# Gated mix of softmax attention and a linear-attention branch: the fraction step of VectorE's score batches on GpSimd, apart from two-port VectorE operations, and a new order

## The chip, the cores and the metric

The kernel runs on one core of one Trainium2 chip. The metric is the device time of one execution in microseconds (us). Before the change the median of three runs is 838.36 us (837.57 to 838.61). Stretches of the program are read from one profiled execution.

## The reference, cut to what matters

Sequence S = 2048, width 512, 32 heads of 16 numbers, bf16 inputs.

```python
qkv = x @ wqkv                                  # branch A, per head q, k, v
p = softmax(einsum("bhqd,bhkd->bhqk", q, k) * Dh ** -0.5)
a = einsum("bhqk,bhkd->bhqd", p, v) @ wo

phi = lambda u: concat([softmax(u @ w_phi), softmax(-(u @ w_phi))])   # branch B
kv, z = einsum("bhsf,bhsd->bhfd", phi(k), v), sum_s(phi(k))
b = (einsum("bhqf,bhfd->bhqd", phi(q), kv) / (phi(q) . z + 1e-6)) @ wo_B

g = sigmoid((x * gate_w).sum(-1))
out = g * a + (1 - g) * b
```

Nearly all of the work is branch A: 32 heads of 2048 x 2048 scores, an exponential of each, and the product with v.

## The kernel before, in words

**Tiles and packs.** The scores are cut into 2048 units: a unit is one head, 128 keys by 512 queries. Four units (four heads, on four row groups of TensorE) are a pack; 512 packs run in order, in 32 groups of 16 packs (the 16 key blocks of four heads and one query chunk). One pack lasts about 1.6 us.

**Two ways for the exponential.** Most units go the ScalarE way: `_qk` (L1001) writes their scores into a ring of five PSUM banks, `_exp` (L1027, the activation at L1035) takes 3 and 2 units by turns and writes ET, and `_pv` (L1042, L1104) multiplies ET with V. The units in `self.away` go the VectorE way. `_plan_vector` (L831) chooses them: SHARES[g] of them in group g, spread over the 14 packs behind the group's first (in the last group over ENDS places), always the fourth head of a pack; four more (SOON) are fixed by hand. They are gathered in batches of NB = 5 (the first two have 2, the last ones fewer).

**A batch on VectorE** (`_vector_batch`, L862): per unit a score matmul (`vqk`) into one of three PSUM banks outside the ring, and an evacuation `v_bits` (L883) that scales the scores into uint32 in the tile vt, which has two buffers. Then, for all units of the batch at once, `_cubic` (L902): `v_frac` (L907) takes one byte of each number, a fraction, into vf as fp16; `v_line` (L909), `v_sq` (L910) and `v_cube` (L911) make a cubic polynomial of it; and `v_out` (L893) adds the exponent and writes bf16 bits into vu. TensorE multiplies vu with V in a step of its own (`pvx`, L1104, vu).

**Other work of VectorE.** Evacuations of projections (L703, L759, L783, L1252, L1268), the norm of each pair of groups (L1157 to L1169), all of branch B's feature map (`_b_part`, L1255, names b_...), and the output (L1489, L1541). GpSimd (the engine POOL) does nothing but a few fills and small steps in the first 24 us.

**What sets the order.** All operations are listed with an engine, a planned cost, dependencies, a due time in packs (`prio`) and an earliest time (`rel`). `Plan.order` (L153) plays them through in Python ahead of time with its planned costs and latencies, and picks for the engine that is ready first the operation that is due first. The result is one fixed instruction queue for each engine; `emit` (L286) puts semaphore waits where a dependency crosses engines. At run time each engine works through its queue in order, so an instruction that waits holds all that stand behind it. TensorE's queue also holds padding matmuls (`_fill`, L1109, recorded at L1113) where it would have little to do.

`self.n_bits % 2` chooses the vt buffer. LEAD is by how many packs a batch is due ahead of its first use, QDUE the same for the query projections (`_proj_q`, L751: a projection, an evacuation at L759 and eight small DMAs on SP's queue into qT), K0 and Q0 the start of branch B's key and query steps, KEEP the pack of a group from which a bank is held back for the next group's accumulator.

## Time and profile before

| | us |
|---|---|
| median of three runs | 838.36 |
| span of the profiled execution | 836.5 |
| TensorE busy | 792.9 |
| VectorE busy | 806.8 |
| ScalarE busy | 825.4 |
| GpSimd busy | 8.0 |
| first score activation starts, last one ends | 7.35, 831.64 |
| granted TensorE clock, mean | 1.000 |

The span runs from the first to the last instruction of the profiled execution; it is 1.86 us under the median of the runs. In the lines below, PE is TensorE, PEld its weight loads, DVE is VectorE, ACT is ScalarE, POOL is GpSimd, SP the engine that issues most DMAs. A group line gives the line of the code, engine, operation, output <- input, shapes and count, then the busy time and the mean time of one in ns, then how long the engine sat idle just before these instructions and what ended that. A line of a stretch gives its bounds, its length and then for PE, PEld, DVE, ACT and POOL the busy time and the number of instructions. A timeline line gives start and length in us. Instructions that follow each other on an engine overlap a little in these records: one that reads PSUM on VectorE is listed with 0.68 us while the next starts 0.60 us later.

### The profile page before, as it was taken

Reading aid. Unit: us, or ns where it says so; the run is one execution under the profiler, and the core shown is the slowest. Engines: PE = TensorE matmul, PEld = TensorE weight load, DVE = VectorE, ACT = ScalarE, POOL = GpSimd, SP = SyncE. Lnnn points to the kernel's source line nnn. Section 1 sums busy time; section 2 is a strip of 40 time slices with the busy share of each in tenths; the row PEclk is TensorE's granted clock in tenths of the full one; section 3 lists DMA queues with packets and bytes.
Section 4 is the critical chain, followed back from the end, with each engine's and each line's share of the span. In section 5 each row is a group of like instructions: output and inputs, shape, how many; then the busy total and the mean of one; then the engine's idle time right before and its main releaser. Section 6 shows DMA issues by size and latency. Waiting matters only on the chain.

```text
span 836.5 us, 19540 instructions
## 1 busy us (share of the span) xinstructions
PE 792.9 (95%) x8711; PEld 263.0 (31%) x8753; DVE 806.8 (96%) x1050; ACT 825.4 (99%) x733; POOL 8.0 (1%) x15
## 2 busy tenths in 40 slices
PE   9999999999999999999999999999999999999998
PEld 4323333333232222232223322222322223222234
DVE  6999999999999999999999999999998999999994
ACT  7999999999999999999999999999999999999997
POOL 3000000000000000000000000000000000000000
PEclk9999999999999999999999999999999999999999
DMA  9500000000000000210003010003100003000000
GB/s 250 157 6 8 1 7 1 2 1 8 2 7 2 7 1 8 52 22 13 1 7 59 20 33 2 4 5 70 27 15 8 1 11 79 21 8 2 2 2 27
DMA packets 49027, 20.01 MB, mean 24 GB/s; under 512 B 38704, under 2 KB 48944, under 8 KB 48944
## 3 DMA queue, kind: packets, MB, share of 16 engines
q1 hardware_dynamic: 48272, 18.58, 9.4%
q8 instruction: 68, 1.11, 0.6%
q10 hardware_dynamic: 672, 0.20, 0.1%
q14 instruction: 15, 0.12, 0.0%
HBM read 6.31 MB, written 2.10 MB: 10 GB/s over the span
## 4 chain that ended last, share of the span: by engine, by line
ACT 92%; DVE 5%; PE 2%; DMA 0%; SPq 0%; issue 0%
ACT ET L1035 92%; DVE vt L883 1%; PE ps L984 0%; DMA qT<-qraw 0%; SPq L761 0%; PE ps L633 0%; DVE vu L893 0%; PE ps L1113 0%; DVE bq L1268 0%; DVE vt L1321 0%; DVE VB L1252 0%; DVE T L1157 0%; DVE vf L907 0%; DVE vu L911 0%; DVE vf L910 0%; DVE bq L1315 0%
## 5 line engine op out<-in xcount | busy, mean ns | idle before, releaser
L1035 ACT ACTIVATE ET<-ps 128x1536 bf16<-128x1536 f32 x728 | 823.1, 1397 | 1.7 <-PE ps L984 1.5
L984 PE MATMUL ps<-qT,kT 32*128 32x512 bf16 (+2 forms) x2249 | 318.4, 364 | 31.4 <-ACT ET L1035 22.2
L1113 PE MATMUL ps<-kT,zero 128*32 128x512 bf16 (+1 forms) x3052 | 255.3, 383 | 0.0
L1104 PE MATMUL ps<-ET,V 128*32 128x512 bf16 (+2 forms) x1998 | 195.8, 364 | 1.3 <-ACT ET L1035 0.6
L984 PEld LDWEIGHTS ps<-qT,kT 32*128 32x128 bf16 x2249 | 83.5, 91 | 305.5 <-ACT ET L1035 227.1
L883 DVE TENSOR_SCALAR vt<-ps 128x512 uint32<-128x512 f32 x226 | 148.3, 681 | 3.8 <-PE ps L984 3.1
L893 DVE SCALAR_TENSOR_TENSOR vu<-vt,vu 128x2560 int16<-128x2560 uint32 (+3 forms) x47 | 127.6, 2716 | 0.7
L1113 PEld LDWEIGHTS ps<-kT,zero 128*32 128x32 bf16 x3052 | 67.9, 94 | 103.2 <-issue 78.5
L1104 PE MATMUL ps<-vu,V 128*32 128x512 bf16 (+1 forms) x250 | 85.3, 364 | 0.3 <-DVE vu L893 0.3
L1104 PEld LDWEIGHTS ps<-ET,V 128*32 128x32 bf16 x1998 | 55.0, 95 | 67.0 <-issue 36.9
L910 DVE TENSOR_TENSOR vf<-vf 128x2560 f16<-128x2560 f16 (+3 forms) x49 | 68.6, 1400 | 0.6
L911 DVE TENSOR_TENSOR vu<-vu,vf 128x2560 f16<-128x2560 f16 (+3 forms) x49 | 68.5, 1398 | 0.5
L907 DVE TENSOR_SCALAR vf<-vt 128x2560 f16<-128x2560 uint8 (+3 forms) x47 | 67.1, 1427 | 0.2
L681 PE MATMUL ps<-WB,xT 128*128 128x512 bf16 x165 | 48.8, 383 | 4.0 <-issue 1.6
L909 DVE TENSOR_SCALAR vu<-vf 128x2560 f16<-128x2560 f16 (+3 forms) x49 | 37.9, 774 | 2.0 <-PE ps L1104 1.8
L681 PE MATMUL ps<-xT,WA 128*128 128x512 bf16 (+1 forms) x124 | 35.8, 380 | 0.0
L1157 DVE STREAM_TRANSPOSE T<-ps 128x512 f32<-128x512 f32 (+1 forms) x35 | 23.2, 664 | 5.0 <-PE ps L1104 4.6
L1104 PEld LDWEIGHTS ps<-vu,V 128*32 128x32 bf16 x250 | 22.9, 96 | 11.5 <-issue 8.5
L681 PEld LDWEIGHTS ps<-WB,xT 128*128 128x128 bf16 x192 | 14.4, 97 | 27.0 <-issue 14.3
L1268 DVE TENSOR_SCALAR bq<-ps 128x512 bf16<-128x512 f32 x32 | 21.5, 679 | 0.5 <-PE ps L681 0.4
L777 PE MATMUL ps<-WA,xT 128*128 128x128 bf16 x256 | 18.9, 220 | 0.4 <-DVE vt L883 0.2
L1321 DVE TENSOR_TENSOR vt<-vt,brec 128x4096 bf16<-128x4096 bf16 (+1 forms) x10 | 18.6, 1857 | 0.0
(105 smaller groups left out, 421.8 us busy)
## 6 DMA issues: line engine op xcount, KB each, us to landing
qT<-qraw SPq DMA_DIRECT2D x120, 16.0 KB, 1.8
xn<-in_A_x_dram SPq DMA_DIRECT2D x3, 512.0 KB, 6.1
WB<-in_B_wqkv_dram SPq DMA_DIRECT2D x3, 512.0 KB, 5.0
out_dram<-WB SPq DMA_DIRECT2D x12, 128.0 KB, 1.9
WA<-in_A_wqkv_dram SPq DMA_DIRECT2D x3, 384.0 KB, 5.2
xn<-in_A_x_dram SPq DMA_DIRECT2D x2, 256.0 KB, 3.6
WoA<-in_A_wo_dram SPq DMA_DIRECT2D x1, 512.0 KB, 5.7
WoB<-in_B_wo_dram SPq DMA_DIRECT2D x1, 512.0 KB, 6.6
```

Of the source, the lines that this page charges most:

```text
L681: mm = op("PE", lambda e, c=c: e.matmul(self._bank(job)[:, 0:n], lhs(c), rhs(c), start=(c == 0), stop=(c == 3)), self.c_pe(n), reads=reads ...
L883: parts.append(op("DVE", lambda e, j=j, job=job: e.tensor_scalar(vt[:, j, :], self._bank(job), SCALE * LOG2E * 2.0 ** 24, 2.0 ** 31, op0=A ...
L893: o = op("DVE", lambda e: e.scalar_tensor_tensor(out=flat(vu).bitcast(I16), in0=flat(vt), scalar=2.0 ** -17, in1=flat(vu), op0=ALU.mult, o ...
L907: ("_frac", two, lambda e: e.tensor_scalar(vf, frac, 1 / 256, ROOT, op0=ALU.mult, op1=ALU.add), [b_vt], [b_vf]),
L909: lambda e: e.tensor_scalar(vu, vf, CUBE, SQUARE, op0=ALU.mult, op1=ALU.add), [b_vf], [b_vu]),
L910: ("_sq", two, lambda e: e.tensor_tensor(vf, vf, vf, ALU.mult), [b_vf], [b_vf]),
L911: ("_cube", two, lambda e: e.tensor_tensor(vu, vu, vf, ALU.mult), [b_vf, b_vu], [b_vu]),
L984: ins = e.matmul(out[u][:, cols], self.kT[32 * i:32 * i + 32, cp, kt * TOK:(kt + 1) * TOK], self.qT[32 * i:32 * i + 32, s, q], start=True, ...
L1035: o = plan.op("ACT", lambda e: e.activation(self.ET[:, a % NS:a % NS + n, :], self.ps[:, a % NR:a % NR + n, :], ACT.Exp, scale=SCALE), sel ...
L1104: ins = e.matmul(self._bank(ot)[32 * i:32 * i + 32, to], self.V[:, kt, g8 // 2, v0:v0 + 32], tile[:, cols], start=first and j == 0, stop=o ...
L1113: ins = e.matmul(self._bank(ot)[32 * i:32 * i + 32, lo:QCH], self.zero[:], self.kT[:, 0, lo:QCH], start=False, stop=False, tile_position=( ...
L1157: return e.transpose(to, acc if alone else acc.rearrange("p (e b d) -> p e b d", e=2, b=8))
```

## The change

Four things change.

1. `v_frac` goes from VectorE to GpSimd in all batches but the two SOON ones and the last two (TAIL). It is the same operation (one byte of each uint32 in, fp16 out), with a planned cost of 0.2 + 0.00138 n us for n numbers. It depends on the `v_out` of the batch before (`last_out`).
2. The planner keeps a set PORT of operation names: those of VectorE that read two tensors from SBUF or copy within SBUF in a fast mode. `order` places no such VectorE operation beside a GpSimd `v_frac`: each gets a dependency, and so a semaphore wait, on the last one of the other engine (GIVE 0.15 and TAKE 0.12 are the planned gaps), and a VectorE operation of the set that would start less than GUARD ahead of a booked `v_frac` is planned behind it. `v_bits`, all other evacuations from PSUM, the 32x32 transposes and the reciprocals are not in the set; `b_octave` (L1321), which reads two SBUF tensors, is not either.
3. The score matmuls of a batch wait for `v_cube` (SOONER) of the batch that last used their vt buffer and no longer for its `v_out`; the evacuation into vt still waits for `v_out`.
4. SHARES sums to 231 instead of 226 and is spread anew; LEAD, QDUE, VPRIO, TPRIO, KEEP, ENDS, K0 and Q0 get new values. With these, and with the new costs, the whole order of all queues is computed anew.

```diff
+    PORT = {"v_frac", "v_line", "v_sq", "v_cube", "v_out", "gate_z", "gate_h", "gate_b", "n_den", "n_mul", "kvbd", "b_grid", "b_rest",
+            "b_max", "b_top", "b_down", "b_square", "b_slope", "b_even", "b_odd", "b_part", "b_out", "b_sum", "b_ratio", "b_mul"}
+    GUARD, GIVE, TAKE = 0.25, 0.15, 0.12
...
+            pool = [(max(free["POOL"], o.dep_t, port["DVE"].end + self.GIVE if port["DVE"] else 0.0), o) for o in avail["POOL"]
+                    if o.port and o.rel <= self.now]
+            booked = min(pool, key=lambda x: x[0]) if pool else None
...
+                    if o.port and e == "POOL" and port["DVE"]:
+                        t = max(t, port["DVE"].end + self.GIVE)
+                    elif o.port and e == "DVE":
+                        if port["POOL"]:
+                            t = max(t, port["POOL"].end + self.TAKE)
+                        if booked and t > booked[0] - self.GUARD:
+                            t = max(t, booked[0] + booked[1].cost + self.TAKE)
...
+            if o.port and e in port:
+                other = port["DVE" if e == "POOL" else "POOL"]
+                if other is not None:
+                    o.deps.append(other)
+                port[e] = o
...
-    NB, NVU, LEAD = 5, 3, 13
-    QDUE, VPRIO, VREL, TPRIO = 28.0, -16.0, 161.0, 5
-    KEEP = 14
+    NB, NVU, LEAD = 5, 3, 14
+    QDUE, VPRIO, VREL, TPRIO = 32.9152, -18.5545, 161.0, 3
+    KEEP = 15
...
-    ENDS = 9
+    ENDS = 11
+    POOL = 0.00138
+    SOONER = "_cube"
+    TAIL = 2
...
-    SHARES = (0, 2, 2, 6, 0, 5, 4, 5, 8, 4, 9, 9, 10, 4, 15, 4,
-              2, 14, 8, 8, 12, 3, 6, 7, 14, 8, 7, 12, 6, 11, 14, 7)
+    SHARES = (0, 2, 2, 8, 0, 5, 5, 2, 9, 4, 11, 8, 12, 3, 13, 4, 4, 11, 7, 11, 8, 6, 8, 10, 14, 6, 4, 14, 6, 10, 14, 10)
...
-                   reads=self._score_bufs([u]), deps=b_vt.readers, name="vqk", prio=due + step * j, rel=due + step * j - self.VREL, kind="row",
+                   reads=self._score_bufs([u]), deps=b_vt.soon or b_vt.readers, name="vqk", prio=due + step * j, rel=due + step * j - self.VREL, kind="row",
...
-                op0=ALU.mult, op1=ALU.add), self.c_dve(512), deps=[m], name="v_bits",
+                op0=ALU.mult, op1=ALU.add), self.c_dve(512), deps=[m, *b_vt.readers], name="v_bits",
...
-            op("DVE", fn, cost, reads=reads, writes=writes, name="v" + name, prio=prio)
-        o = op("DVE", lambda e: e.scalar_tensor_tensor(
+            pool = name == "_frac" and not soon and number < len(self.batches) - self.TAIL
+            o = op("POOL" if pool else "DVE", fn, 0.2 + n * self.POOL if pool else cost, reads=reads, writes=writes, name="v" + name,
+                   prio=prio, deps=[self.last_out] if pool else ())
+            if name == self.SOONER:
+                b_vt.soon = [o]
+        self.last_out = o = op("DVE", lambda e: e.scalar_tensor_tensor(
...
-    K0, SK, Q0, SQ = 17.0, 8.5, 178.25, 18.0
+    K0, SK, Q0, SQ = 16.878, 8.5, 178.0371, 18.0
```

More of the change, by code (lines that the diff above doesn't have):

```diff
@@ L32, in __init__ @@
         self.readers = []
+        self.soon = []
 class Job:
@@ L66, in __init__ @@
         self.strips = (None, ())
+        self.port = name in Plan.PORT
 class Plan:
@@ L165, in order @@
         queues = {e: [] for e in self.ENGS}
+        port = {"DVE": None, "POOL": None}
         left = len(self.ops)
@@ L884, in _vector_batch @@
                 vt[:, j, :], self._bank(job), SCALE * LOG2E * 2.0 ** 24, 2.0 ** 31,
-                op0=ALU.mult, op1=ALU.add), self.c_dve(512), deps=[m], name="v_bits",
+                op0=ALU.mult, op1=ALU.add), self.c_dve(512), deps=[m, *b_vt.readers], name="v_bits",
                 prio=due + step * j - 40, release=job))
-        b_vt.writers, b_vt.readers = parts, []
+        b_vt.writers, b_vt.readers, b_vt.soon = parts, [], []
         self.last_bits = parts
@@ L918, in _attention @@
         self.n_bits = 0
+        self.last_out = None
         self._plan_vector()
@@ L1277, in _b_part @@
         b_vt, b_vf = self.b_vt[k], self.b_vf
+        b_vt.soon = []
         two, four = lambda n: 0.057 + n * 0.000525, lambda n: 0.066 + n * 0.000262
```

## The prediction

> **What bounds the kernel now.** I read the busy times first, then the chain that ended last, then the groups by shape, then stretches of VectorE.

> ```profile
> PE 792.9 (95%) x8711; PEld 263.0 (31%) x8753; DVE 806.8 (96%) x1050; ACT 825.4 (99%) x733; POOL 8.0 (1%) x15
> ...
> ACT 92%; DVE 5%; PE 2%; DMA 0%; SPq 0%; issue 0%
> ...
> L1035 ACT ACTIVATE ET<-ps 128x1536 bf16<-128x1536 f32 x728 | 823.1, 1397 | 1.7 <-PE ps L984 1.5
> ```

> ScalarE does nothing but exponentials from 7.35 us (start of the first) to 831.6 us, and waits 1.7 us in all between them. So it sets the end, and only fewer tiles on it, or less of the fixed 7.35 us before and 4.9 us behind, shorten the kernel. The same view by shape:

> ```profile
> L1035 ACT ACTIVATE ET<-ps 128x1536 bf16<-128x1536 f32 x364 | 585.8, 1609 | 0.9 <-PE ps L984 0.8
> L1035 ACT ACTIVATE ET<-ps 128x1024 bf16<-128x1024 f32 x363 | 430.4, 1186 | 0.8 <-PE ps L984 0.7
> ...
> L1035 ACT ACTIVATE ET<-ps 128x512 bf16<-128x512 f32 x1 | 0.8, 752 | 0.0
> ```

> These are 3, 2 and 1 tiles: 3 x 364 + 2 x 363 + 1 = 1819 of 2048, so 229 tiles are elsewhere. VectorE evacuates 230 score tiles: SHARES has a 15 for 14 places, and one tile is made twice. VectorE is the second limit: how many tiles it can take decides how many ScalarE can lose. Its stretches:

> ```profile
> 20.00:205.00 185.00, 178.85 (x1717) 63.87 (x1730) 181.00 (x299) 185.00 (x166) 0.26 (x1) 1.00 0.08 24
> 205.00:615.00 410.00, 388.89 (x4210) 118.64 (x4225) 406.37 (x483) 408.99 (x363) 0.00 (x0) 1.00 0.08 18
> 615.00:820.00 205.00, 193.97 (x2352) 63.51 (x2359) 200.97 (x226) 204.94 (x182) 0.00 (x0) 1.00 0.06 14
> ```

> The columns are PE, PEld, DVE, ACT, POOL. In the middle 410 us VectorE is busy 406.4 us: no tile could be added there without relief.

> **Tiles off ScalarE.** The new SHARES sum to 231, with SOON 235, and no group has more tiles than places; so 235 differ, six more than now. ScalarE keeps 1813 = 3 x 363 + 2 x 362: one activation of 3 tiles, one of 2 and one of 1 go. 1.609 + 1.186 = 2.80 us is more than a pair takes, since activations overlap: (823.1 - 0.5) / 363.5 = 2.26 us a pair, so 0.27 us of each lies under the next. The single one is worth 0.752 - 0.27 = 0.49 us. Gain: 2.26 + 0.49 = **2.75 us**, all on the path.

> **The end.** The last activation is now one tile; it becomes three. Behind the single one TensorE does 16 products in 0.41 us, behind three it does 48, which took 0.87 us at 829.4 us. Cost 0.46 us. The last group loses three more tiles (7 to 10, reaching two packs further); its two last batches keep the fraction on VectorE, which has been idle in most of the last 16.5 us (5.8 us busy), so I cost that at nothing; a late last batch would show one for one.

> **Query loads earlier.** The one wait of ScalarE that lies in mid kernel is 0.70 us at 247.4 us, behind a query copy (L759) that was late on a full VectorE. QDUE from 28 to 32.9 asks for that copy about five packs, 8 us, earlier: gain 0.7 us, bounds 0 and 1.5.

> **Relief of VectorE.**

> ```profile
> L883 DVE TENSOR_SCALAR vt<-ps 128x512 uint32<-128x512 f32 x226 | 148.3, 681 | 3.8 <-PE ps L984 3.1
> L893 DVE SCALAR_TENSOR_TENSOR vu<-vt,vu 128x2560 int16<-128x2560 uint32 x43 | 121.2, 2818 | 0.6
> ...
> L907 DVE TENSOR_SCALAR vf<-vt 128x2560 f16<-128x2560 uint8 x43 | 63.6, 1478 | 0.2
> ```

> Batches: 43 of five become 44; those and two of 1024 elements give their fraction step (L907) to GpSimd: 46 operations. VectorE loses 43 x 1.478 + 2 x 0.688 = 64.9 us and gains 5 x 0.681 us of evacuation and one batch of 0.81 + 1.48 + 1.48 + 2.82 = 6.6 us: net -55 us, 806.8 to about 752. The price is the waits.

> **Price of the GpSimd operation.** The trace has none of this form. Nearest rows:

> ```profile
> L571 POOL MEMSET qT<- 128x2048 bf16 x1 | 1.8, 1804 | 0.0
> ...
> L574 POOL TENSOR_TENSOR wphi<-wphin,heads 128x512 bf16<-128x512 bf16 x1 | 1.1, 1051 | 1.5 <-DMA wphin<-in_B_w_phi_dram 1.5
> ```

> 0.88 ns an element with no input and 2.05 ns with two: 2.3 to 5.25 us for 2560 elements. One input lies between; the planner books 0.2 + 2560 x 0.00138 = 3.73 us, the middle of the bounds, which I take. With its gaps of 0.15 and 0.12 us a window is 4.0 us in which VectorE may run only operations outside PORT. The trace shows one handover, GpSimd to VectorE, 0.03 us after the recorded end (1.47 to 1.50 us), so I do not add to the gaps.

> [...]

> **What lies beside the window.** The wait is in VectorE's in-order queue: behind a waiting port operation stand evacuations, and TensorE, in order too, waits for their banks with ScalarE's next scores behind. Only work placed ahead of it covers. The trace shows what is at hand just behind v_out, where a window will open:

> ```profile
> 618.21 2.83 DVE L893 SCALAR_TENSOR_TENSOR vu<-vt,vu 128x2560 int16<-128x2560 uint32 x1
> 620.95 1.49 DVE L907 TENSOR_SCALAR vf<-vt 128x2560 f16<-128x2560 uint8 x1
> 622.36 2.54 DVE L883 TENSOR_SCALAR vt<-ps 128x512 uint32<-128x512 f32 x4
> 625.44 0.69 DVE L759 CAST qraw<-ps 128x512 bf16<-128x512 f32 x1 [0.54 <-PE ps L681]
> 626.04 0.68 DVE L883 TENSOR_SCALAR vt<-ps 128x512 uint32<-128x512 f32 x1
> ```

> From 622.36 to 626.7 us VectorE does 4.3 us of PSUM reads, all outside PORT, for the next batch: that is the window, ready made. In the middle stretch I split VectorE's groups by PORT. Outside: L883 85.0, transposes 11.4, L1268 10.8, L1321 9.1, L1438 8.0, other evacuations, reciprocals and small ones 24.4, sum 149 to 154 us; inside, without L907: the batches' four steps 165.4, the rest about 80. Listed times overlap by 7% (437 listed, 406.4 busy). With some six tiles more: outside 147, batches 161, the rest 75 us net, sum 383 of 410. About 27 windows take 109 us. So 27 us are to spare, and **the windows must be at least 75% filled** ((109 - 27) / 109). The 147 us are enough for that, and the run above fills one wholly. In the last 205 us the same sum gives about 180 us, and 55% is enough; ahead of 205 us windows are few. So I take the waits as absorbed: cost 0, bounds 0 and the rival's below.

> Looser waits of the vqk scores (on v_cube, not v_out) cost nothing: no more TensorE work, and the evacuations waited 3.1 us for scores at most. TensorE has the room for the extra single products, as L1113 shows: 255 us of it is padding.

> **Sum.** 836.5 - 2.75 + 0.46 - 0.7 = 833.5 us of span. The median of the runs is 838.36, 1.86 above the span; carried over: **835.4 us**, -0.35%. About 0.2%, 1.7 us, is what a measurement of this kernel can tell from no change, so the margin is thin.

> **Rivals.**
> (a) *Small new waits eat the gain.* A new order has places where VectorE is a little late, as at 247 us now. For it: almost every L984 load waits for ScalarE by under 1 us, so there is little depth. Against: one such order left only 1.7 us. Three of 0.7 us give 837.5; within 836.7 to 840.0. Chance 0.18.
> (b) *The windows are too long: slower.* The order is written for 3.73 us. With windows 85% full, 27 - 16 = 11 us are spare in the middle; over 27 windows that is 0.4 us each, so it decides from a GpSimd operation of 4.1 us (4.7 if they are full). At 4.6 us: (0.87 - 0.4) x 27 = 13 us late, 848; at the two-input row's 5.25 us, 30 us, 865; just over the point, 841. For it: the row of 2.05 ns an element. Against: one input only. Likeliest 844. Chance 0.22.
> (c) *b_octave meets GpSimd.* L1321 reads two SBUF tensors but its name is not in PORT, so the order may put it into a window; 2.29 us each, five of the six long ones behind 200 us. If GpSimd holds what it needs, it ends up to 3.7 us late; ScalarE has about one activation (1.1 us) ahead, so 2.6 us are lost each time; three give 835.4 + 7.8 = 843. For it: it is long and always ready behind port operations. Against: 27 us are spare. Chance 0.06.
> [...]

> That the change does not do what it says is possible only in the count: it is six tiles, not five, and is in the sum.

> **Chances.** Forecast 0.54 (own range 833.5 to 836.6: the query wait's bounds and an end that costs nothing or 1 us), (a) 0.18, (b) 0.22, (c) 0.06. Faster 0.54, same 0.18, slower 0.28. The range goes from 833.5 to 846, which leaves out the upper part of (b).

> **What would show it.** Right: 363 and 362 activations, ScalarE waiting under 2.5 us in all, GpSimd operations of 3.6 to 4.0 us, VectorE busy near 752 us, and behind each v_out evacuations up to the next L909. Wrong: ScalarE waiting on TensorE that waits on L883, L909 waiting long on GpSimd, or L1321 longer than 2.29 us.

## The result and the profile after

The changed kernel takes 841.36 us, median of five runs (839.71 to 841.87), against 838.07 us (837.57 to 838.61) for the kernel before in the same comparison: a ratio of 1.0038 [1.0027, 1.0048]. It is 0.38% **slower**, where 0.35% faster was forecast. The profiled execution took 841.87 us, with a span of 840.1 us.

Line numbers have moved: the score matmul is now L1012 (was L984), the activation L1063 (L1035), the padding L1141 (L1113), v_bits L906 (L883), v_out L920 (L893), v_frac L934 (L907), v_line L936 (L909). The page of the changed kernel:

```profile
PE 796.0 (95%) x8483; PEld 262.9 (31%) x8528; DVE 761.7 (91%) x1014; ACT 823.5 (98%) x730; POOL 112.4 (13%) x61
...
PEclk9999999999999999999999899988999999999999
...
ACT 90%; PE 7%; DVE 3%; issue 0%; DVEq 0%
...
L1063 ACT ACTIVATE ET<-ps 128x1536 bf16<-128x1536 f32 x725 | 821.2, 1392 | 6.5 <-PE ps L1012 6.2
L1141 PE MATMUL ps<-kT,zero 128*32 128x512 bf16 (+1 forms) x2828 | 237.7, 387 | 0.0
...
L936 DVE TENSOR_SCALAR vu<-vf 128x2560 f16<-128x2560 f16 (+3 forms) x50 | 38.9, 777 | 0.4 <-POOL vf L934 0.4
```

Two lines of the page before stand against these:

```profile
PEclk9999999999999999999999999999999999999999
...
L1113 PE MATMUL ps<-kT,zero 128*32 128x512 bf16 (+1 forms) x3052 | 255.3, 383 | 0.0
```

VectorE is relieved, and the GpSimd operation is waited for by 0.4 us at v_line, so the new handover costs nothing there. ScalarE still sets the end, but its share of the chain fell from 92 to 90% and TensorE's rose from 2 to 7%: ScalarE now waits 6.5 us for scores instead of 1.7. The line that is easy to pass over is PEclk. It was 9 in every slice before; now three slices show an 8, about half way through and after. There is also less padding: 2828 products at L1141, where 3052 were issued before.

The activations by shape are the ones forecast, 363 of 3 tiles and 362 of 2:

```profile
L1063 ACT ACTIVATE ET<-ps 128x1536 bf16<-128x1536 f32 x363 | 582.2, 1604 | 4.2 <-PE ps L1012 4.1
L1063 ACT ACTIVATE ET<-ps 128x1024 bf16<-128x1024 f32 x362 | 426.8, 1179 | 2.3 <-PE ps L1012 2.1
```

The stretches, with the columns PE, PEld, DVE, ACT, POOL and then the granted clock (1.00 is full):

```profile
205.00:615.00 410.00, 388.07 (x4015) 117.22 (x4032) 370.47 (x452) 404.58 (x358) 58.12 (x25) 0.98 0.08 18
615.00:820.00 205.00, 195.06 (x2211) 62.53 (x2215) 189.75 (x215) 205.00 (x183) 34.88 (x15) 1.00 0.07 14
```

VectorE's load in the middle stretch fell from 406.4 to 370.5 us, and still ScalarE lost 4.4 us there. I took the start of every activation against that of the next, less the usual period (1.344 us for three tiles, 0.918 for two), and added it up by 50 us. Before the change the sum is at most 0.4 us everywhere but from 200 to 250 us, where it is 1.0. After, all but two of the sums are at most 0.7 us: 2.5 us come from 450 to 500 us and 4.4 us from 550 to 600. Short stretches, the first line from the first of these two places, the others from the second:

```profile
465.00:470.00 5.00, 5.00 (x65) 1.76 (x61) 4.30 (x7) 4.74 (x5) 0.00 (x0) 0.64 0.02 3
555.00:560.00 5.00, 4.66 (x59) 1.39 (x56) 5.00 (x4) 5.00 (x6) 0.00 (x0) 1.00 0.01 3
560.00:565.00 5.00, 3.33 (x27) 0.62 (x23) 4.21 (x5) 5.00 (x6) 0.00 (x0) 0.70 0.00 0
565.00:570.00 5.00, 5.00 (x37) 0.95 (x37) 3.11 (x4) 3.63 (x3) 0.00 (x0) 0.50 0.00 0
```

Read the number of matmuls beside the clock. From 555 to 560 us TensorE runs 59; from 560 to 565 us only 27, while ScalarE is still busy all the time; then the clock is at one half. TensorE is now "busy" for all of 565 to 570 us, with 37 matmuls that take longer each, and only there does ScalarE fall behind. So in time the order is: few matmuls, lower clock, late scores. Single lines show the same (start, length; x is the number of matmuls merged into a line):

```profile
558.47 1.35 PE L1012 MATMUL ps<-qT,kT 32*128 32x512 bf16 x7
...
560.34 0.39 PE L1012 MATMUL ps<-qT,kT 32*128 32x512 bf16 x2
561.68 0.39 PE L1012 MATMUL ps<-qT,kT 32*128 32x512 bf16 x3 [0.96 <-ACT ET L1063]
562.60 0.60 PE L1012 MATMUL ps<-qT,kT 32*128 32x512 bf16 x2 [0.53 <-ACT ET L1063]
```

The groups of two or three matmuls have the bracketed waits for ScalarE between them, and the same two side by side go from 0.39 to 0.60 us. In the whole execution the clock is at one half from 466.4 to 473.2 us, 562.0 to 572.2 and 592.7 to 596.1: 20.5 us, in pieces of one, two and three times 3.41 us, and full otherwise.

The five runs of the changed kernel carry the argument one step further, since their order is the same and only the clock differs. Time at half clock is 2 x (1 - mean clock) x span: 13.4 us in two runs with spans of 837.8 us, 16.8 us in two with 839.2 and 839.4, 20.2 us in the one with 840.1. A line through them has a slope of 0.36 us for each us at half clock and meets zero at **833.1 us**. The forecast span was 833.5 us.

### The profile page after: what moved, and what is told of

The parts are those of the page before. It is cut to its first block, busy times and chain, and to the rows that moved or that the text cites. A ratio compares the mean times of both kernels' runs of the same rounds, so it can differ in the third digit from the quotient of the medians.

```text
span 840.1 us, 19126 instructions
## 1 busy us (share of the span) xinstructions
PE 796.0 (95%) x8483; PEld 262.9 (31%) x8528; DVE 761.7 (91%) x1014; ACT 823.5 (98%) x730; POOL 112.4 (13%) x61
## 4 chain that ended last, share of the span: by engine, by line
ACT 90%; PE 7%; DVE 3%; issue 0%; DVEq 0%
ACT ET L1063 90%; PE ps L1012 2%; PE ps L1132 1%; PE ps L1141 1%; PE ps L705 1%; DVE vt L906 1%; PE ps L657 0%; PE ps L801 0%; DVE vu L920 0%; PE ps L1264 0%; DVE vf L937 0%; PE ps L1478 0%; DVE vu L938 0%; DVE WB L1518 0%; DVE V L807 0%
## 5 line engine op out<-in xcount | busy, mean ns | idle before, releaser
L1063 ACT ACTIVATE ET<-ps 128x1536 bf16<-128x1536 f32 x725 | 821.2, 1392 | 6.5 <-PE ps L1012 6.2
L1012 PE MATMUL ps<-qT,kT 32*128 32x512 bf16 (+2 forms) x2248 | 324.3, 367 | 33.2 <-ACT ET L1063 25.2
L1141 PE MATMUL ps<-kT,zero 128*32 128x512 bf16 (+1 forms) x2828 | 237.7, 387 | 0.0
L1132 PE MATMUL ps<-ET,V 128*32 128x512 bf16 (+2 forms) x1983 | 198.3, 369 | 0.8 <-DVE T L1185 0.3
L934 POOL TENSOR_SCALAR vf<-vt 128x2560 f16<-128x2560 uint8 (+1 forms) x46 | 104.4, 2269 | 675.9 <-DVE vu L920 340.2
L1012 PEld LDWEIGHTS ps<-qT,kT 32*128 32x128 bf16 x2248 | 84.5, 91 | 310.9 <-ACT ET L1063 233.8
L906 DVE TENSOR_SCALAR vt<-ps 128x512 uint32<-128x512 f32 x231 | 151.2, 683 | 33.3 <-PE ps L1012 30.2
L920 DVE SCALAR_TENSOR_TENSOR vu<-vt,vu 128x2560 int16<-128x2560 uint32 (+3 forms) x48 | 130.2, 2713 | 0.5
L1141 PEld LDWEIGHTS ps<-kT,zero 128*32 128x32 bf16 x2828 | 62.5, 95 | 98.4 <-issue 76.4
L1132 PE MATMUL ps<-vu,V 128*32 128x512 bf16 (+1 forms) x265 | 85.4, 362 | 0.0
L1132 PEld LDWEIGHTS ps<-ET,V 128*32 128x32 bf16 x1983 | 55.6, 96 | 64.3 <-issue 36.5
L938 DVE TENSOR_TENSOR vu<-vu,vf 128x2560 f16<-128x2560 f16 (+3 forms) x50 | 70.3, 1405 | 0.5
L936 DVE TENSOR_SCALAR vu<-vf 128x2560 f16<-128x2560 f16 (+3 forms) x50 | 38.9, 777 | 0.4 <-POOL vf L934 0.4
L1132 PEld LDWEIGHTS ps<-vu,V 128*32 128x32 bf16 x265 | 23.3, 96 | 19.3 <-issue 13.4
L705 PEld LDWEIGHTS ps<-WB,xT 128*128 128x128 bf16 x192 | 14.1, 97 | 25.8 <-issue 13.6
L1350 DVE TENSOR_TENSOR vt<-vt,brec 128x4096 bf16<-128x4096 bf16 (+1 forms) x10 | 18.6, 1857 | 0.0
```

The lines of the kernel that those rows point to most:

```text
L705: mm = op("PE", lambda e, c=c: e.matmul(self._bank(job)[:, 0:n], lhs(c), rhs(c), start=(c == 0), stop=(c == 3)), self.c_pe(n), reads=reads ...
L906: parts.append(op("DVE", lambda e, j=j, job=job: e.tensor_scalar(vt[:, j, :], self._bank(job), SCALE * LOG2E * 2.0 ** 24, 2.0 ** 31, op0=A ...
L920: self.last_out = o = op("DVE", lambda e: e.scalar_tensor_tensor(out=flat(vu).bitcast(I16), in0=flat(vt), scalar=2.0 ** -17, in1=flat(vu), ...
L934: ("_frac", two, lambda e: e.tensor_scalar(vf, frac, 1 / 256, ROOT, op0=ALU.mult, op1=ALU.add), [b_vt], [b_vf]),
L936: lambda e: e.tensor_scalar(vu, vf, CUBE, SQUARE, op0=ALU.mult, op1=ALU.add), [b_vf], [b_vu]),
L938: ("_cube", two, lambda e: e.tensor_tensor(vu, vu, vf, ALU.mult), [b_vf, b_vu], [b_vu]),
```

## The experiments

**Theory A:** TensorE has lulls in the new order; in each of them the clock is halved for a few us, TensorE is then too slow for ScalarE, and that is the loss. **Theory B** (the rivals of the prediction, taken together): the waits around the GpSimd operation and the new order itself make VectorE or TensorE late, and the clock only follows. To place the lulls I estimated from the matmul records how full TensorE's array is: the part of the 128x128 array that a product uses (32 of 128 rows, or of 128 columns, is a quarter) by the time its columns take, which the plan books at 0.2133 us for 512; in the trace of before products of 128x128x512 that follow each other most often start 0.216 us apart. In the 3.41 us ahead of the three falls of the clock this was 0.37, 0.30 and 0.26; in the kernel before it is nowhere under about 0.39.

**1. The same order, its lulls filled.** Nothing is moved; 33 score groups in lulls of the plan get one extra product of 128x128x512 ahead of them, into the bank that the scores then overwrite.

```diff
-            for o in p.order()["PE"]:
+            p.order()
+            self._lulls()
+            for o in p.queues["PE"]:
...
+    LOW, MOST = 0.45, 1
+    def _lulls(self):
...
+                share = sum(w + (self.plan.FILL * o.filled if o.name.startswith("qk") else 0) for s, w, o in work if t <= s < t + 3.413) / 3.413
+                if share < self.LOW and a.filled < self.MOST and (best is None or share < best[0]):
...
+            best[1].filled += 1
```

> The changed kernel's order, with nothing moved: one more 128x128x512 product (0.21 us) is put ahead of each of 33 score groups, where the planned order leaves TensorE's array under 45% full over 3.4 us. Theory A (the array's lulls halve the granted clock, and the half clock makes ScalarE wait): granted clock 1.000 in place of 0.988, ScalarE's idle time before L1063's activations from 6.5 to 1 to 2 us, median 841.4 - 5.2 = about 836. Theory B (ScalarE waits because VectorE and its banks are late in the new order; the clock only follows): the clock may rise, ScalarE's waits stay over 5 us, median 840 to 842, or above for the added products.

Measured: 837.93 us, median of 12 runs (836.90 to 844.20), against 838.10 us before: 1.001 [0.9993, 1.0027]. In the profiled run, of 840.25 us, one of the two places is mended and the other is not:

```profile
465.00:470.00 5.00, 4.70 (x77) 2.21 (x80) 4.41 (x8) 4.89 (x5) 0.77 (x1) 1.00 0.06 19
560.00:564.00 4.00, 3.40 (x15) 0.64 (x15) 3.12 (x4) 3.76 (x5) 0.00 (x0) 0.59 0.00 0
564.00:568.00 4.00, 4.00 (x27) 0.78 (x30) 2.10 (x3) 3.12 (x4) 0.00 (x0) 0.50 0.00 0
```

At 465 us the clock stays full and the loss of 450 to 500 us falls from 2.5 to 0.1 us; at 560 us the clock falls as before and 3.6 us are lost. The runs sort themselves by the clock: six at a mean of 1.000 have spans of 835.1 to 835.5 us, two at 0.998 have 836.7 and 836.8, two at 0.994 have 838.4 and 839.4, one at 0.992 has 840.7 and one at 0.990 has 842.3. One program, the same waits, 7 us apart: 0.40 us for each us at half clock. Theory A has the cause of this spread; B has nothing that differs between these runs. The runs at a full clock lie near the 836 us that A expected (836.9 to 837.3); a clock of 1.000 in every run, which A expected too, did not come. The half clock comes in some runs and not in others, with one order for all, so the order alone does not decide it.

**2. Lulls made in the kernel before.** Its order, tiles and constants, with the padding left out in three stretches of 9 us of the plan.

```diff
+            p.queues["PE"] = [o for o in p.queues["PE"] if o.name != "pad" or not any(a < o.start < a + 9 for a in (300, 450, 600))]
```

> The kernel before, its order kept, without the padding products in three stretches of 9 us (at 300, 450 and 600 us of the plan), which leaves the array about 25 to 35% full there; nothing waits longer by it. Theory A: two or three stretches at half clock, of 3.4 to 10 us each, and 1 to 2 us of ScalarE waiting in each: median 840 to 843. Theory B: padding is only padding: clock about 1.000 or lower without harm, median within 0.2% of 838.1.

Measured: 850.67 us (849.84 to 851.37), 1.0149 [1.0136, 1.0162]. The kernel before, and then this one, in the first of the three places:

```profile
307.00:314.00 7.00, 6.62 (x82) 2.06 (x84) 7.00 (x6) 7.00 (x8) 0.00 (x0) 1.00 0.00 0
314.00:321.00 7.00, 6.78 (x70) 2.02 (x66) 6.97 (x17) 7.00 (x7) 0.00 (x0) 1.00 0.01 2
```

```profile
307.00:314.00 7.00, 5.23 (x48) 1.44 (x47) 6.86 (x6) 6.60 (x6) 0.00 (x0) 0.85 0.00 0
314.00:321.00 7.00, 7.00 (x40) 1.03 (x38) 4.18 (x7) 4.95 (x4) 0.00 (x0) 0.50 0.00 0
```

Work that nobody reads is left out, and 2.05 of 7 us of ScalarE are lost from 314 to 321 us. The clock is at one half for 13.7, 10.2 and 10.2 us, 34.1 in all, for 12.6 us more: 0.37 us each, close to the 0.36 of the changed kernel. Theory A had the sign and the mechanism; the size came out far above the 840 to 843 that I had expected, because I had expected 1 to 2 us of waiting at each fall; the sums by 50 us show 5.2, 3.4 and 3.9. The padding is not spare time here: in the three stretches without it the clock fell, and with it the clock was full.

**3 and 4. The move alone, in the order before.** Order, tiles and constants of the kernel before; the fraction step of 45 batches goes to GpSimd and gets the waits of the change (with b_octave among them). In the second of these kernels APART is False: the waits are left out and nothing else differs.

```diff
+    APART = True
+    def _move(self):
...
+            if o.name == "v_frac" and 2 < done < len(self.batches) - 1:
+                o.eng = "POOL"
+                o.deps += [last] * self.APART
...
+                if pool is not None and self.APART:
+                    o.deps.append(pool)
```

> The kernel before in its own order, tiles and parameters, with only the fraction step of 45 batches handed to GpSimd, and with the waits that keep it apart from VectorE operations on two SBUF ports (b_octave among them). Theory A: GpSimd and its waits do no harm by themselves: operation 2.33 us, VectorE busy about 745 us, clock 1.000, median 837 to 840. Theory B: the waits cost: this order was written for 1.40 us on VectorE, and where v_line stands right behind the fraction step VectorE stands still 1.2 us or more; with half of 45 places that is 25 us, ScalarE waits over 5 us, median above 843.

> The same without the waits that keep them apart (the waits for data stay), so that GpSimd's fraction step and VectorE operations on two SBUF tensors run at the same time in the stretches of branch B. If the two lock each other out: GpSimd operations of over 2.33 us (up to 4 or 5), or VectorE rows of 1.22 and 1.48 us up to 2.3 us longer, in some ten places, and a median like that of the run with waits. If they do not: every duration as before, and VectorE's waits for GpSimd shorter; median no higher than with waits.

Measured with the waits: 849.82 us (847.34 to 850.48), 1.0134 [1.0121, 1.0147]. VectorE is down to 752.1 us, and yet:

```profile
DVE vu L936 <- POOL vf L934: 24.0, 19, 2.4
...
ACT ET L1062 <- PE ps L1011: 9.7, 17, 1.0
```

(time, times, longest one). In this order too little that may run beside GpSimd stands ahead of v_line in 19 of the batches, so it waits 24 us. Here theory B has a part of its own: the move without a new order costs 12 us, of which the clock, 13.6 us at one half, would explain about 5 at the rate above. The padding is all there, 3052 products as before, and the clock still falls twice: the number of them alone does not decide. Measured without the waits: 864.87 us (862.18 to 865.74), 1.0314 [1.03, 1.0327]. First the fraction step with the waits (shortest, median and longest in ns), then without:

```profile
L934 POOL TENSOR_SCALAR vf<-vt x45: 1044/2324/2326, 29.9 to 804.0; 128x2560 f16<-128x2560 uint8 x43, 128x1024 f16<-128x1024 uint8 x2
```

```profile
L934 POOL TENSOR_SCALAR vf<-vt x45: 1044/3233/4968, 29.5 to 815.9; 128x2560 f16<-128x2560 uint8 x43, 128x1024 f16<-128x1024 uint8 x2
```

```profile
544.44 2.83 DVE L920 SCALAR_TENSOR_TENSOR vu<-vt,vu 128x2560 int16<-128x2560 uint32 x1
544.49 4.96 POOL L934 TENSOR_SCALAR vf<-vt 128x2560 f16<-128x2560 uint8 x1 [6.73 <-DVE vu L938]
```

A GpSimd operation that starts 0.05 us behind a v_out of 2.83 us ends 2.2 us behind it: it takes about 2.7 + 2.3 us, as if it did nothing until v_out was done. The trace has 19 such places (0.03 to 0.17 us behind a v_out, 4.83 to 4.97 us long). It also has the other order: where v_out starts behind the GpSimd operation, it is v_out that takes 4.22 to 4.94 us, nine times. That is the waits' reason, and they are worth 15 us in this order, a time for which I had no expectation; about 4 of these go with 10 us more at half clock.

**5. The lulls filled further.** As the first, with up to two products ahead of a group, 54 in all.

```diff
-    LOW, MOST = 0.45, 1
+    LOW, MOST = 0.48, 2
```

> The changed kernel's order again, with 54 added products ahead of 36 score groups (up to two ahead of one), chosen where the planned array is under 48% full. The run with 33 kept one stretch at half clock behind 557 us and its times spread from 836.9 to 844. Theory A: no stretch at half clock, every run near the lowest of the run with 33, median 836.5 to 837.5 (54 products of 0.21 us mostly hidden while ScalarE is busy). Theory B: the added products delay scores and it is slower than the run with 33, above 838.

Measured: 841.29 us (840.70 to 841.48) against 837.63, 1.0040 [1.0027, 1.0054]. The clock was at 1.000 in all five runs, as A expects, and the time no better than the changed kernel's, as B expects. ScalarE's gaps are few, but its activations are busy for 823.1 us for 1813 tiles (821.2 in the changed kernel). Their starts, added up as above, are 5.9 us late in many small pieces, of which none in 50 us is over 1.5; in the changed kernel everything outside its two places adds up to nothing. The likely reason is that the added products stand ahead of scores for which ScalarE has little depth; I did not try to part this further. What follows is that products laid in the way of the scores give back what the clock saves: at a full clock 33 of them left spans of about 835.2 us and 54 left 838.8 to 839.7, against 833.1 by the line above.

**6. The new tiles and constants without GpSimd.** All fraction steps stay on VectorE; the order is computed anew.

```diff
-            pool = name == "_frac" and not soon and number < len(self.batches) - self.TAIL
+            pool = False
```

> The changed kernel with its tiles (235) and parameters, the fraction step kept on VectorE in all batches, the order computed anew. What the move to GpSimd is worth at this number of tiles: VectorE has about 64 us more to do and cannot keep up; ScalarE waits 7 us or more in all, median 842 to 846 with the clock at 0.99 to 1.00. If the move to GpSimd is what harms the changed kernel: 836 to 838.

Measured: 842.88 us (842.70 to 843.13), 1.0062 [1.0048, 1.0076], at a clock of 1.000. VectorE is busy 814.8 us, 97%.

```profile
ACT ET L1063 <- PE ps L1132: 4.3, 2, 2.9
ACT ET L1063 <- PE ps L1012: 2.2, 3, 1.4
```

With 235 tiles off ScalarE and no relief, two waits of 2.9 and 1.5 us, at 91.8 and 202.0 us, end with a value product (L1132), while the last score products had ended 2.2 and 1.0 us before. TensorE's own waits for VectorE just ahead of them are 0.6 us at most, so what made these value products late is not shown. The move to GpSimd by itself is not what made the change slow: without it these tiles are slower still, in an order of their own, and with a full clock.

**7 and 8. Other orders of the same change.** The GpSimd step and its waits are kept. Its planned cost is the measured one (0.2 + 2560 x 0.00083 = 2.32 us), the score matmuls wait for v_out as before the change, and SHARES and the other constants are drawn anew; of the orders that came out I took two by how full the array is planned to be. The first has 237 tiles off ScalarE and no planned 3.4 us under 41%. The second has 236, and five added products of the kind above.

```diff
-    NB, NVU, LEAD = 5, 3, 14
-    QDUE, VPRIO, VREL, TPRIO = 32.9152, -18.5545, 161.0, 3
-    KEEP = 15
+    NB, NVU, LEAD = 5, 3, 11
+    QDUE, VPRIO, VREL, TPRIO = 37.87721735122653, -15.777585606589676, 115.32266234197697, -16
+    KEEP = 14
...
-    ENDS = 11
-    POOL = 0.00138
-    SOONER = "_cube"
+    ENDS = 7
+    POOL = 0.00083
+    SOONER = "_none"
...
-    SHARES = (0, 2, 2, 8, 0, 5, 5, 2, 9, 4, 11, 8, 12, 3, 13, 4, 4, 11, 7, 11, 8, 6, 8, 10, 14, 6, 4, 14, 6, 10, 14, 10)
+    SHARES = (0, 2, 6, 4, 0, 3, 8, 0, 8, 7, 10, 9, 7, 10, 9, 10, 3, 11, 13, 7, 10, 3, 8, 5, 13, 10, 0, 13, 14, 12, 14, 4)
...
-    K0, SK, Q0, SQ = 16.878, 8.5, 178.0371, 18.0
+    K0, SK, Q0, SQ = 16.685246443552867, 9.175636919541722, 179.5852095783672, 18.37640428698314
```

> GpSimd's fraction step kept, its planned cost set to what the trace shows (0.2 + 2560 x 0.00083 = 2.325 us), the score products waiting for v_out as before, and another order: 237 tiles off ScalarE, chosen so that no stretch of 3.4 us of the planned order leaves TensorE's array under 41% full. Theory A: granted clock 1.000, ScalarE's idle before L1063's activations under 2.5 us, and the gain of eight tiles against the kernel before (three pairs and two, 3.6 us): median 834 to 835.5. Theory B (moving the step to GpSimd makes ScalarE wait, whatever the array does): ScalarE's waits over 5 us, median 838 or above.

> The same with a third order: 236 tiles off ScalarE, nearly none of them in the last group, and five added products where the planned array is under 42% full. Theory A: clock 1.000, median 834 to 836. Theory B: 838 or above.

Measured, the first: **833.65 us** (833.42 to 834.32) against 837.74, 0.995 [0.9936, 0.9964], faster than both kernels. Its page:

```profile
PEclk9999999999999999999999999999999999999999
...
L1063 ACT ACTIVATE ET<-ps 128x1536 bf16<-128x1536 f32 x725 | 819.3, 1383 | 0.8 <-PE ps L1012 0.7
...
L1141 PE MATMUL ps<-kT,zero 128*32 128x512 bf16 (+1 forms) x3044 | 251.4, 383 | 0.0
```

The padding is back at 3044 products, the clock at full in every slice, and ScalarE waits 0.8 us. From the kernel before its activations fall from 823.1 to 819.3 us, 3.8 us for eight tiles: 0.475 us a tile, where the prediction's 2.75 us for six makes 0.46. The second: 835.67 us (834.57 to 838.25), 0.9979 [0.997, 0.9988]. Its three runs at a clock of 1.000 have spans of 832.7 to 833.1 us; the eight others, with 3.3 to 10 us at half clock, have 833.8 to 836.4: 0.32 us for each. In the profiled one the clock falls once, at 811.9 us, beyond the 805 us up to which I had looked for lulls.

## Why the prediction was wrong

**The step that failed** stands at the end of the part on the window: "TensorE has the room for the extra single products, as L1113 shows: 255 us of it is padding." I read padding as room. It is what held the clock up: with three stretches of 9 us of it left out, kernel 2 was at half clock for 34.1 us. The new order issues 224 fewer of these products and leaves lulls that none of them fill. "Sum" then had no term for the clock, which the profile of before showed at 1.000 throughout, and I took it for given. The PEclk row was there to be read; I did not ask what kept it at 9. The price: 20.5 us at half clock in the profiled execution, at 0.36 us each 7.3 us, which the sums by 50 us (2.5 + 4.4, and little beside them) match. Without them the line through the five runs gives 833.1 us of span, 0.4 us under the forecast.

Point by point:

- *Tiles off ScalarE*: right in count (363 and 362 activations) and in size. The trace adds up: 0.1 us more ahead of the first activation, 2.75 less for the tiles, 5.7 more of late starts (6.8 against 1.1, added up as above) and 0.5 more behind the last one make 3.5 us of span, as measured. The busy time fell by only 1.9 us; I take the rest for overlap that each new wait breaks up. The order with a full clock has 0.475 us a tile.
- *The end*: from the last activation's end to the span's end it is 5.39 us, was 4.90: 0.49 us more, 0.46 forecast.
- *Query loads earlier*: the wait at 247 us is gone; the sum for 200 to 250 us went from 1.0 to -0.2 us. The first 50 us lost 0.6, which no term had.
- *Relief of VectorE*: 761.7 us, 752 forecast. VectorE is relieved, by 10 us less, and it did not matter: v_bits now waits 30 us for scores, so VectorE has time over. The forecast had subtracted listed times, which overlap by 7% as the prediction itself says; that is about 4 of the 10 us.
- *Price of the GpSimd operation*: 2.325 us for 2560 elements, 0.91 ns each; 3.73 was taken, within bounds of 2.3 and 5.25, and it lies at their lower end, on the row with no input. It was mis-sized by 60%. No wait for GpSimd came of it, but the order was written for windows 1.4 us longer than they are, and whether that has a part in the lulls was not tried by itself.
- *What lies beside the window*: held, for windows of 2.3 us instead of 3.7. VectorE waited for GpSimd 0.4 us at v_line and 1.8 us each at two steps of branch B. The example at 622 us holds 3.9 us of reads, not 4.3; the rest of it is a wait for TensorE.
- *Looser waits of the vqk scores*: "no more TensorE work" is true, but the padding moved; kernel 6 has this edit and keeps a full clock, so it does not make the lulls alone, and whether it has a part in them was not tried.

**The rivals.** (b), the long windows, and (c), b_octave, did not occur: the operation was short, and L1350, the old L1321, is at 2284 ns in its long form (2285 before); none of its ten ran beside a v_frac, so what such a meeting would cost was not seen. (a) named small new waits at 837.5 us; there were waits, but in two places, and behind a half clock instead of a late VectorE. That 841 us also stands in (b), for an operation just over its point, is chance.

**What stays open.** In the planned order, at the lulls, all three banks outside the ring are taken: one by the finished group's accumulator, which waits for VectorE's last tiles and its transpose, two by vqk scores that VectorE can evacuate only when v_out is done. With no bank for the next group's accumulator there can be neither value products nor padding. This is read from the order and was not tried. Which edit made the lulls is open too. Not the tiles and constants by themselves (kernel 6 keeps a full clock), and not the GpSimd step by itself (kernel 7 has it and keeps a full clock); the whole order decides.

## What to carry to other kernels

Before you count idle or padded TensorE time as room, ask what it does for the clock: look at the granted clock beside the number of matmuls in stretches of a few us, and put a term for it into the sum. When a kernel has several times from one program, sort its runs by mean clock first; if the time goes with it, the loss is there and not in the order's waits. An operation moved to another engine needs an order written around it: the same move cost 1.3% in the old order, 0.4% in the order of the change and gained 0.5% in a third (the last two with six and eight more tiles off ScalarE).

## What the runs showed of the hardware

**GpSimd.** One pass from every fourth byte to fp16 with an arithmetic step took 0.91 ns an element over 2560 elements, 1.57 times the 1.478 us that VectorE took for the same step, and beside evacuations from PSUM its time did not vary (44 of them in the changed kernel, 2324 to 2327 ns). Started just behind a v_out, which reads two tensors from SBUF, it ended as late as if it had waited for that one's end (19 places of kernel 4, 4.83 to 4.97 us instead of 2.33); where it started ahead of v_out, it was v_out that took longer (nine times, 4.22 to 4.94 us; 4.22 us instead of 2.83 at one place where GpSimd took its usual 2.32). Through what they meet no run shows: "two-port" in the title and "two SBUF ports" in the expectation of kernel 3 are names for the VectorE operations that are kept apart. Of the "fast mode" in the second point of the change the trace of before shows that v_line took 0.81 us for the 2560 numbers for which v_frac took 1.48 on VectorE.
